# Cross-attention into a maxout FFN on one core: another order of loads, transposes, G pairs and first-layer slices

## The chip, the cores and the metric

The kernel runs on one core of a Trainium2 chip. The metric is the device time of one execution in microseconds (us); lower is better. Four runs of the kernel before took 165.84 to 167.21 us, with a median of 166.62 us.

## What is computed

The reference in short, for x of shape (8, 8, 512, 64) (batch, head, token, width) and state of shape (8, 8, 32, 64):

```python
a     = softmax(x @ state.T / 8)        # per batch and head: 512 x 32
xread = a @ state                       # 512 x 64
a2    = softmax(state @ x.T / 8)        # 32 x 512
sread = a2 @ x                          # 32 x 64
y     = concat([xread, sread])          # per batch 544 rows, heads side by side: 512 columns
h     = max(y @ w1, y @ w2, y @ w3)     # each w is 512 x 768
out   = h @ w_out                       # 4352 x 512, float32
```

## The kernel before, in words

**A rewrite of the first layer.** For the token rows, `xread @ w` is computed as `a @ (state @ w)`. The product `state @ w`, called G, is made per batch by `g_cols` (L230, matmuls L239). One call makes G for one or two of the six 128-column slices m of d_ff; a slice covers the three weights, so it has 384 columns for each of two groups g of heads. Each slice goes into one PSUM tile of tag `two` and is copied to SBUF by ScalarE (L245), or later, when it is deferred into `copies_due` (the copy is then taken up inside the next `maxout`, L265).

**A batch b** passes through these helpers. `load_x` (L68) brings x as bf16 through POOL's queue. The transpose of x is made by TensorE (`x_transpose`, L143) or by a DMA transpose on SP's queue (`x_transpose_dma`, L155). `scores` (L159) multiplies it with the block-diagonal states `bd` into a PSUM tile of tag `two` (or two halves of tag `pw`), and ScalarE takes the exponential (L176) straight out of that tile. `softmax` (L178) is a sum and a reciprocal on VectorE (L183, L185) and a multiply on POOL or VectorE (L186). The transpose of a is again TensorE's (`a_transpose`, L191) or a DMA's (`a_transpose_dma`, L200). `sread` (L207) makes the state rows. `x_maxout(b, m)` (L270, through `maxout`, L253) is one first-layer slice: six matmuls of 128x512 into three PSUM tiles of tag `pw` (L260), a copy of the first to SBUF by ScalarE (L264), and two maxima by VectorE with the second and the third (L267, L268). `ffn_out(b, j)` (L280) is the second layer for a quarter of the tokens: six matmuls into one `pw` tile (L285), a ScalarE copy (L292) and, after each second quarter, an output DMA. `s_maxout` (L275) is the first layer for the state rows of all batches, done beside batch 7.

**PSUM.** The pool has two buffers for tag `two`, [128, 1024] float32 [...], and four for tag `pw`[...]. The tile framework makes the first matmul into a buffer wait until the engine that reads the buffer's former tile has finished.

**Order.** The order on every engine is the order of the program text (`manual_schedule`). First comes a start-up with the loads (L56 to L107) and filler matmuls (`keep_busy`). Then comes the dual phase, in which batches 0 and 1 advance together while the weights arrive: their order is written out by hand, and it ends with G of batch 2 complete and two of batch 0's `ffn_out` quarters done. Then follows a loop over b = 2 to 7: `x_maxout(b, m)` for m = 0 to 5, and after each slice m the work in `slots[m]`: the preparation of batch n = b+1 and the `ffn_out` quarters that are still pending. At the end come the last quarters of batch 7 and of the state rows. The POOL queue carries the loads of x (from batch 1 on), of the weights and of states 1 to 3, most output DMAs, and POOL's softmax multiplies, all in program order; the SP queue carries the DMA transposes.

Lines that the change and the prediction touch:

```python
chunks = ((0, 1), (1, 3), (3, 6))                                    # d_ff slices of a weight load
pp = ctx.enter_context(tc.tile_pool(name="pp", bufs=2, space=bass.MemoryType.PSUM))
p = pp.tile([128, J, n, HS, Ns], F32, tag="two", name="ps")          # scores
p = pp.tile([128, 2, 512], F32, tag="two", name="pg")                # G
p = pp.tile([128, 512], F32, tag="pw", bufs=4, name=f"pw{i}")        # first layer
```

Of the kernel before, what the change touches and what calls it, by code (L numbers as in the profile page):

```python
# [8 lines left out]
F32 = mybir.dt.float32  # L9
BF16 = mybir.dt.bfloat16  # L10
# [5 lines left out]
def kernel(  # L16
# [14 lines left out]
    nc = tc.nc  # L31

    B, H, S, D = x.shape
# [19 lines left out]
    ctx.enter_context(tc.manual_schedule())  # L53

# [29 lines left out]
    for b in range(B):  # L84
        nc.gpsimd.memset(x_sb[b][:, XW:XW + D], 1.0)

    chunks = ((0, 1), (1, 3), (3, 6))
# [3 lines left out]
    def load_w(c):  # L91
        m0, m1 = chunks[c]
        for i, w in enumerate((moe_w1, moe_w2, moe_w3)):
            nc.gpsimd.dma_start(  # L94
                out=w_sb[c][:, :, i, :],
                in_=w.rearrange("(kk p) f -> p kk f", p=128)[:, :, m0 * 128:m1 * 128])
# [6 lines left out]
    load_w(0)  # L103
    bds = [data.tile([128, 2, H, 2, Ns], BF16, name=f"bd{k}") for k in range(B // 2)]
    nc.vector.memset(bds[0], 0.0)
    load_x(1)
    load_w(1)  # L107
# [19 lines left out]
    def states(k, copy):  # L127

        p = pp.tile([128, 4, 128], BF16, tag="pw", bufs=4, name="pt")
        for t in range(4):  # L130
            nc.tensor.transpose(p[:, t, :], st[k][:, t].rearrange("p c d -> p (c d)"), ident)  # L131
        for c in range(2):
            r = slice(64 * c, 64 * c + 64)
            copy(out=bds[k][r, :, :, c, :].rearrange("p b h (q t) -> p (b h) q t", t=4),  # L134
                 in_=p[r].rearrange("p t (k q) -> p k q t", q=8))
# [93 lines left out]

    def g_cols(b, ms, copies=(nc.scalar.copy, nc.scalar.copy), defer=(False, False)):  # L230

        for m, copy, wait in zip(ms, copies, defer):
# [47 lines left out]
    def ffn_out(b, j, split=False):  # L280
# [7 lines left out]
        if split:  # L288
            nc.scalar.copy(out=o[:, j, 0:256], in_=p[:, 0:256])
            nc.vector.tensor_copy(out=o[:, j, 256:512], in_=p[:, 256:512])  # L290
        else:
            nc.scalar.copy(out=o[:, j, :], in_=p)  # L292
# [17 lines left out]
    dve, act, pool = nc.vector.tensor_copy, nc.scalar.copy, nc.gpsimd.tensor_copy  # L310
    both = (True, True)
# [11 lines left out]
    load_w(2)  # L323
    load_x(2)
    nc.gpsimd.dma_start(out=wout_sb, in_=moe_w_out.rearrange("(kk p) f -> p kk f", p=128))
    scores(0, 1, 2)
    softmax(0, 1, 2, nc.vector.tensor_mul)
    g_cols(0, (0,))
    keep_busy(4)
    a_transpose(0, 0, act)  # L330
    a_transpose(0, 1, dve)
    x_transpose(1, 0, act)
    x_transpose(1, 1, dve)
    x_maxout(0, 0)
    scores(1, 0, 2)
    softmax(1, 0, 2, nc.gpsimd.tensor_mul)
    for k in range(1, B // 2):
        load_st(k, nc.gpsimd)
    load_x(3)
    sread(0)  # L340
    g_cols(0, (1, 2))
    x_maxout(0, 1)
    g_cols(1, (0, 1), defer=both)
    a_transpose(1, 0, act)
    a_transpose(1, 1, dve)
    x_maxout(0, 2)
    sread(1)
    x_maxout(1, 0)
    g_cols(1, (2,))
    x_maxout(1, 1)  # L350
    g_cols(0, (3, 4), defer=(False, True))
    states_cast(1, pool)
    x_maxout(1, 2)
    x_maxout(0, 3)
    g_cols(1, (3, 4), defer=both)
    x_maxout(0, 4)
    states(1, dve)
    x_transpose(2, 0, dve)
    x_transpose(2, 1, dve)
    x_maxout(1, 3)  # L360
    g_cols(0, (5,), defer=both)
    scores(2, 0, 2)
    softmax(2, 0, 2, nc.gpsimd.tensor_mul)
    x_maxout(1, 4)
    g_cols(1, (5,), defer=both)
    states_cast(2, pool)
    states_cast(3, pool)
    x_maxout(0, 5)
    sread(2)
    x_maxout(1, 5)  # L370
    g_cols(2, (0, 1))
    a_transpose(2, 0, act)
    a_transpose(2, 1, dve)
    ffn_out(0, 0)
    g_cols(2, (2, 3))
    ffn_out(0, 1)
    g_cols(2, (4, 5))
    assert not copies_due


    pending = [(0, 2), (0, 3)] + [(1, j) for j in range(J)]
    for b in range(2, B):
        n = b + 1
        slots = [[] for _ in range(NM)]
        if n < B:
            if n == 3:
                slots[0].append(lambda: x_transpose(n, 0, act))
                slots[0].append(lambda: x_transpose(n, 1, dve))
                slots[3].append(lambda: x_transpose_dma(n + 1))
            elif n + 1 < B:  # L390
                slots[0].append(lambda: x_transpose_dma(n + 1))
            at = 1 if n == 3 else 0
            slots[at].append(lambda: scores(n, 0, 2))
            slots[at].append(lambda: softmax(n, 0, 2, nc.gpsimd.tensor_mul))
            slots[2 if n == 3 else 1].append(lambda: g_cols(n, (0, 1)))
            slots[2].append(lambda: a_transpose_dma(n))
            slots[3].append(lambda: sread(n))
            slots[4].append(lambda: g_cols(n, (2, 3)))
            slots[5].append(lambda: g_cols(n, (4, 5)))
            slots[4].append(late_transposes)  # L400
            if n % 2 and n + 1 < B:
                slots[3].append(lambda: states((n + 1) // 2, act))
            for k in ((4, 5) if n == 3 else (n + 2,)):
                if k < B:
                    slots[0].append(lambda k=k: load_x(k))
# [3 lines left out]
        for m in (1, 2, 3, 4, 5) if len(pending) > 4 else (1, 2, 4, 5):  # L409
            if pending:  # L410
                slots[m].append(lambda t=pending.pop(0): ffn_out(*t))
# [4 lines left out]
        pending += [(b, j) for j in range(J)]  # L416
    assert pending == [(B - 1, j) for j in range(J)]
# [36 lines left out]
```

The softmax here doesn't subtract the row's maximum and nothing guards it: scores larger than these inputs give would overflow.

## Time and profile before

| | |
|---|---|
| median of 4 runs | 166.62 us |
| the profiled execution | 166.23 us, span of the trace 164.4 us, mean TensorE clock 0.985 |
| busy: TensorE, ScalarE, VectorE, POOL | 151.3, 99.1, 95.9, 43.9 us |
| first G matmul (first weight chunk there) | 9.52 us |
| first slice of batch 0, of batch 2 | 13.60 us, 46.48 us |
| first slices of batches 3, 4, 5, 6, 7 | 65.27, 82.68, 99.24, 115.37, 131.50 us |
| last matmul group issued, end of span | about 160.2 us, 164.4 us |

The profile is of one execution. "PE" is TensorE's matmuls, "PEld" its weight loads, "DVE" VectorE, "ACT" ScalarE; L260 is a line of the kernel. In the timeline a line has the start (us), the duration, the engine, the source line, the operation, its operands and how many were merged; in brackets stands the idle time of the engine just before, and what ended it. The modelled end of a matmul runs over the next one's start, so the time that a group takes on TensorE is read from start to start.

### The profile page before, as it was taken

How to read it: one execution, taken by the hardware profiler on the slowest of the kernel's cores; microseconds unless marked ns; L12 is line 12 of the kernel's file. 1: busy time of each engine (PE TensorE's matmuls, PEld its weight loads, DVE VectorE, ACT ScalarE, POOL GpSimd, SP SyncE). 2: the span in 40 equal slices, each digit the busy share in tenths (PEclk: the TensorE clock that was granted, in tenths of full speed). 3: DMA queues.
4: the chain of work that ended last, by engine and by line, in shares of the span. 5: the costliest groups of instructions: out<-in, count | busy, mean ns of one | idle time of the engine just before them, and what ended most of it. 6: DMA issues, size and time to landing. Idle time of an engine off the chain costs nothing.

```text
span 164.4 us, 3569 instructions
## 1 busy us (share of the span) xinstructions
PE 151.3 (92%) x1432; PEld 71.7 (44%) x1449; DVE 95.9 (58%) x162; ACT 99.1 (60%) x158; POOL 43.9 (27%) x64
## 2 busy tenths in 40 slices
PE   7869699988999999999999999999999999999990
PEld 2436244533445444444344434444444466665430
DVE  4766777889418553665548464865586455585001
ACT  3337578366896678853876688648755853333440
POOL 8975550106150601081016101410141010100140
PEclk9969999999999999999999999999999999999998
DMA  4999999800039999269993988560306030030373
GB/s 136 188 172 198 203 201 246 128 7 0 0 121 136 137 252 201 56 113 140 277 154 131 128 188 89 180 193 12 128 0 195 8 130 0 0 132 0 128 236 147
DMA packets 31825, 20.94 MB, mean 127 GB/s; under 512 B 17185, under 2 KB 29345, under 8 KB 31809
## 3 DMA queue, kind: packets, MB, share of 16 engines
q0 software_dynamic: 15632, 15.08, 46.7%
q1 hardware_dynamic: 16176, 5.64, 18.7%
q8 instruction: 11, 0.18, 0.4%
q14 instruction: 6, 0.04, 0.1%
HBM read 15.20 MB, written 8.91 MB: 147 GB/s over the span
## 4 chain that ended last, share of the span: by engine, by line
PE 65%; DVE 11%; ACT 10%; DMA 4%; issue 4%; POOL 4%; DVEq 0%; ACTq 0%; POOLq 0%
PE pw L260 34%; PE po L285 20%; PE pg L239 4%; DVE den L183 4%; DVE t L267 3%; ACT e L176 3%; ACT G L245 3%; DVE ht L268 3%; DMA w<-in_moe_w_dram 3%; PE ps L171 2%; ACT t L264 2%; PE psr L216 2%; DMA out_dram<-osb 1%; POOL a L186 1%; ACT osb L292 1%
## 5 line engine op out<-in xcount | busy, mean ns | idle before, releaser
L260 PE MATMUL pw<-aT,G 128*128 128x512 bf16 x288 | 71.2, 379 | 3.6 <-ACT G L245 1.8
L267 DVE TENSOR_TENSOR t<-t,pw 128x512 bf16<-128x512 bf16 (+1 forms) x54 | 35.1, 650 | 41.6 <-ACT t L264 39.9
L285 PE MATMUL po<-wout,ht 128*128 128x512 bf16 x188 | 47.9, 380 | 0.8
L260 PEld LDWEIGHTS <-G 128*128 128x128 bf16 x288 | 26.8, 98 | 36.3 <-issue 5.1
L245 ACT CAST G<-pg 128x768 bf16<-128x768 f32 x48 | 36.5, 805 | 8.9 <-PE pg L239 8.7
L264 ACT CAST t<-pw 128x512 bf16<-128x512 f32 (+1 forms) x54 | 30.5, 566 | 14.1 <-PE pw L260 12.6
L268 DVE TENSOR_TENSOR ht<-t,pw 128x512 bf16<-128x512 bf16 (+1 forms) x54 | 35.5, 658 | 5.6
L292 ACT COPY osb<-po 128x512 f32<-128x512 f32 x33 | 19.4, 587 | 21.2 <-PE po L285 20.7
L285 PEld LDWEIGHTS <-ht 128*128 128x128 bf16 x204 | 18.4, 97 | 23.6 <-issue 4.7
L301 POOL DMA_DIRECT2D out_dram<-osb x14 | 7.8, 558 | 70.2 <-ACT osb L292 64.5
L186 POOL TENSOR_TENSOR a<-e,rden 128x1024 bf16<-128x1024 bf16 (+1 forms) x8 | 14.4, 1800 | 33.6 <-DVE rden L185 19.9
L239 PE MATMUL pg<-w,bd 64*32 64x384 bf16 x384 | 13.1, 332 | 1.8 <-DMA w<-in_moe_w_dram 1.8
L183 DVE TENSOR_REDUCE den<-e 128x32 f32<-128x1024 bf16 (+1 forms) x9 | 9.9, 1095 | 2.6 <-ACT e L176 2.6
L176 ACT ACTIVATE e<-ps 128x1024 bf16<-128x1024 f32 x7 | 7.2, 1024 | 5.8 <-PE ps L171 5.8
L239 PEld LDWEIGHTS <-bd 64*32 64x32 bf16 x384 | 3.7, 89 | 12.4 <-issue 12.4
L260 PE MATMUL pw<-ats,w 128*128 128x256 bf16 x72 | 8.8, 273 | 0.0
L260 PEld LDWEIGHTS <-w 128*128 128x128 bf16 x72 | 7.0, 98 | 2.1
L116 PE MATMUL idle<-zero 128*128 128x512 bf16 x12 | 5.9, 630 | 1.4 <-DVE zero L80 1.2
L94 POOL DMA_DIRECT2D w<-in_moe_w_dram x9 | 6.8, 771 | 0.0
L69 POOL DMA_DIRECT2D x<-in_x_dram x7 | 6.6, 951 | 0.0
L134 ACT COPY bd<-pt 64x512 bf16<-64x512 bf16 x6 | 3.5, 580 | 4.2 <-PE pt L131 4.1
L171 PEld LDWEIGHTS <-xT 128*128 128x128 bf16 x128 | 4.7, 98 | 2.4 <-DVE xT L153 0.8
(42 smaller groups left out, 64.6 us busy)
## 6 DMA issues: line engine op xcount, KB each, us to landing
out_dram<-osb POOLq DMA_DIRECT2D x14, 512.0 KB, 3.6
x<-in_x_dram POOLq DMA_DIRECT2D x7, 512.0 KB, 9.1
w<-in_moe_w_dram POOLq DMA_DIRECT2D x3, 384.0 KB, 10.2
w<-in_moe_w_dram POOLq DMA_DIRECT2D x3, 256.0 KB, 8.2
wout<-in_moe_w_out_dram POOLq DMA_DIRECT2D x1, 768.0 KB, 16.3
x0f<-in_x_dram SPq DMA_DIRECT2D x1, 512.0 KB, 3.8
out_dram<-osb SPq DMA_DIRECT2D x1, 512.0 KB, 2.7
out_dram<-osb SPq DMA_DIRECT2D x2, 256.0 KB, 2.1
```

Source lines behind the costliest of these rows:

```text
L171: nc.tensor.matmul(p[:, 2 * jj:2 * jj + 2, g - g0, s, :], xT[b][:, h, jj, :], bd(b, h).rearrange("p c n -> p (c n)"), start=(g == g0 and s ...
L176: nc.scalar.activation(out=e[b][:, :, g0:g1], in_=p, func=AF.Exp, scale=scale)
L183: nc.vector.reduce_sum(out=den, in_=e[b][:, :, g0:g1], axis=AX.X)
L186: mul(out=a[b][:, :, g0:g1].rearrange("p j g s n -> p j (g s) n"), in0=e[b][:, :, g0:g1].rearrange("p j g s n -> p j (g s) n"), in1=rden.r ...
L239: nc.tensor.matmul(p[32 * s:32 * s + 32, g, 0:384].rearrange("p (i f) -> p i f", i=3), bd(b, 2 * s + g)[64 * g:64 * g + 64, g, :], w[64 * ...
L245: copy(out=G[b][:, :, m * 384:(m + 1) * 384], in_=p[:, :, 0:384])
L260: nc.tensor.matmul(p[:, 0:n], lhs(i, k), rhs(k), start=(k == 0), stop=(k == nk - 1))
L264: nc.scalar.copy(out=t0[:, 0:n], in_=pw[0][:, 0:n])
L267: nc.vector.tensor_max(t1[:, 0:n], t0[:, 0:n], pw[1][:, 0:n])
L268: nc.vector.tensor_max(ht[b][:, m, :], t1[:, 0:n], pw[2][:, 0:n])
L285: nc.tensor.matmul(p, ht[b][:, m, j * 128:(j + 1) * 128], wout_sb[:, m, :], start=(m == 0), stop=(m == NM - 1))
L292: nc.scalar.copy(out=o[:, j, :], in_=p)
```

## The change

The weights come in four chunks instead of three, of 1, 1, 2 and 2 slices, and x of batch 1 is loaded before any of them. Of the second chunk one weight is issued early and two behind the first POOL multiply; the third and fourth chunk stand on POOL's queue behind batch 1's first multiply. The dual phase is written in another order: batch 1's scores and softmax come in halves ahead of the first slice, batch 0 has all four of its `ffn_out` quarters done before the loop, and batch 2 enters the loop with two of its six G slices. In the loop `g_cols(b, (2, 3))` (one copy on ScalarE, one on VectorE) follows the scores in slot 0, `g_cols(b, (4, 5))` stands in slot 2, and `g_cols(n, (0, 1))` with `sread(n)` in slot 4. The `softmax` moves to slot 1. Batch 3's transpose of x, batch 2's transpose of a, and the transposes of states 2 and 3 are done by DMA instead of TensorE; POOL copies those states into `bd`. The last quarter of batch 7 goes out as two separate half tiles, one by ScalarE's DMA queue and one by SP's. `g_cols` first carries out copies that are still deferred.

```diff
...
@@ -81,16 +82,16 @@
     ident = const.tile([128, 128], BF16, name="ident")
     make_identity(nc, ident)
     nc.gpsimd.dma_start(out=x0_sb[1], in_=x0_heads(1))
-    for b in range(B):
-        nc.gpsimd.memset(x_sb[b][:, XW:XW + D], 1.0)
-
-    chunks = ((0, 1), (1, 3), (3, 6))
+    load_x(1)
+
+    chunks = ((0, 1), (1, 2), (2, 4), (4, 6))
     w_sb = [wpool.tile([128, HS, 3, (m1 - m0) * 128], BF16, name=f"w{m0}") for m0, m1 in chunks]
     wout_sb = wpool.tile([128, NM, d_model], BF16, name="wout")
 
-    def load_w(c):
+    def load_w(c, parts=(0, 1, 2)):
         m0, m1 = chunks[c]
-        for i, w in enumerate((moe_w1, moe_w2, moe_w3)):
+        for i in parts:
+            w = (moe_w1, moe_w2, moe_w3)[i]
             nc.gpsimd.dma_start(
                 out=w_sb[c][:, :, i, :],
                 in_=w.rearrange("(kk p) f -> p kk f", p=128)[:, :, m0 * 128:m1 * 128])
@@ -101,10 +102,11 @@
         return w_sb[c], slice(f, f + 128)
 
     load_w(0)
+    for b in range(B):
+        nc.gpsimd.memset(x_sb[b][:, XW:XW + D], 1.0)
+    load_w(1, (0,))
     bds = [data.tile([128, 2, H, 2, Ns], BF16, name=f"bd{k}") for k in range(B // 2)]
     nc.vector.memset(bds[0], 0.0)
-    load_x(1)
-    load_w(1)
 
     warm = const.tile([128, 1], F32, name="warm")
     nc.scalar.activation(out=warm, in_=zero[:, 0:1], func=AF.Exp, scale=1.0)
@@ -126,9 +128,13 @@
 
     def states(k, copy):
 
-        p = pp.tile([128, 4, 128], BF16, tag="pw", bufs=4, name="pt")
-        for t in range(4):
-            nc.tensor.transpose(p[:, t, :], st[k][:, t].rearrange("p c d -> p (c d)"), ident)
+        if k < 2:
+            p = pp.tile([128, 4, 128], BF16, tag="pw", bufs=4, name="pt")
+            for t in range(4):
+                nc.tensor.transpose(p[:, t, :], st[k][:, t].rearrange("p c d -> p (c d)"), ident)
+        else:
+            p = data.tile([128, 4, 128], BF16, name=f"stT{k}")
+            nc.sync.dma_start_transpose(out=p, in_=st[k].rearrange("p t c d -> p (t c d)"))
         for c in range(2):
             r = slice(64 * c, 64 * c + 64)
             copy(out=bds[k][r, :, :, c, :].rearrange("p b h (q t) -> p (b h) q t", t=4),
@@ -227,8 +233,13 @@
 
     copies_due = []
 
+    def flush_copies():
+        while copies_due:
+            copies_due.pop(0)()
+
     def g_cols(b, ms, copies=(nc.scalar.copy, nc.scalar.copy), defer=(False, False)):
 
+        flush_copies()
         for m, copy, wait in zip(ms, copies, defer):
             if m == 0:
                 new(G, b, [128, 2, NM * 384], "G", bufs=3)
@@ -286,10 +297,14 @@
                              start=(m == 0), stop=(m == NM - 1))
         o = osb[b]
         if split:
-            nc.scalar.copy(out=o[:, j, 0:256], in_=p[:, 0:256])
-            nc.vector.tensor_copy(out=o[:, j, 256:512], in_=p[:, 256:512])
-        else:
-            nc.scalar.copy(out=o[:, j, :], in_=p)
+            halves = [work.tile([128, d_model // 2], F32, tag=f"oh{k}", bufs=1, name="oh") for k in range(2)]
+            rows = out[b * SP:b * SP + S, :].rearrange("(p j) f -> p j f", j=J)[:, j, :]
+            act(out=halves[0], in_=p[:, 0:256])
+            nc.scalar.dma_start(out=rows[:, 0:256], in_=halves[0])
+            dve(out=halves[1], in_=p[:, 256:512])
+            nc.sync.dma_start(out=rows[:, 256:512], in_=halves[1])
+            return
+        act(out=o[:, j, :], in_=p)
         if b == "s":
             for k in range(4 * j, 4 * j + 4):
                 r0 = k * SP + S
...
@@ -320,101 +333,97 @@
     x_transpose(0, 1, dve)
     scores(0, 0, 1)
     softmax(0, 0, 1, nc.gpsimd.tensor_mul)
-    load_w(2)
-    load_x(2)
-    nc.gpsimd.dma_start(out=wout_sb, in_=moe_w_out.rearrange("(kk p) f -> p kk f", p=128))
+    load_w(1, (1, 2))
     scores(0, 1, 2)
     softmax(0, 1, 2, nc.vector.tensor_mul)
-    g_cols(0, (0,))
     keep_busy(4)
+    x_transpose(1, 0, act)
+    x_transpose(1, 1, dve)
     a_transpose(0, 0, act)
     a_transpose(0, 1, dve)
-    x_transpose(1, 0, act)
-    x_transpose(1, 1, dve)
+    g_cols(0, (0,))
+    scores(1, 0, 1)
+    scores(1, 1, 2)
+    softmax(1, 0, 1, nc.gpsimd.tensor_mul)
+    load_w(2)
+    softmax(1, 1, 2, nc.vector.tensor_mul)
+    load_w(3)
+    load_st(1, nc.gpsimd)
+    load_x(2)
     x_maxout(0, 0)
-    scores(1, 0, 2)
-    softmax(1, 0, 2, nc.gpsimd.tensor_mul)
-    for k in range(1, B // 2):
+    g_cols(0, (1,))
+    g_cols(1, (0,))
+    sread(0)
+    a_transpose(1, 0, act)
+    a_transpose(1, 1, dve)
+    x_maxout(0, 1)
+    nc.gpsimd.dma_start(out=wout_sb, in_=moe_w_out.rearrange("(kk p) f -> p kk f", p=128))
+    for k in range(2, B // 2):
         load_st(k, nc.gpsimd)
     load_x(3)
-    sread(0)
-    g_cols(0, (1, 2))
-    x_maxout(0, 1)
-    g_cols(1, (0, 1), defer=both)
-    a_transpose(1, 0, act)
-    a_transpose(1, 1, dve)
+    x_maxout(1, 0)
+    g_cols(0, (2, 3), (act, dve))
+    sread(1)
+    g_cols(1, (1,), defer=(True,))
     x_maxout(0, 2)
-    sread(1)
-    x_maxout(1, 0)
-    g_cols(1, (2,))
     x_maxout(1, 1)
-    g_cols(0, (3, 4), defer=(False, True))
+    g_cols(1, (2, 3), defer=(False, True))
+    x_maxout(0, 3)
     states_cast(1, pool)
+    g_cols(0, (4, 5), defer=(False, True))
     x_maxout(1, 2)
-    x_maxout(0, 3)
-    g_cols(1, (3, 4), defer=both)
     x_maxout(0, 4)
-    states(1, dve)
+    states(1, act)
     x_transpose(2, 0, dve)
-    x_transpose(2, 1, dve)
+    x_transpose(2, 1, act)
+    x_maxout(0, 5)
+    g_cols(1, (4, 5), defer=(False, True))
     x_maxout(1, 3)
-    g_cols(0, (5,), defer=both)
+    x_transpose_dma(3)
     scores(2, 0, 2)
+    ffn_out(0, 0)
+    x_maxout(1, 4)
     softmax(2, 0, 2, nc.gpsimd.tensor_mul)
-    x_maxout(1, 4)
-    g_cols(1, (5,), defer=both)
-    states_cast(2, pool)
-    states_cast(3, pool)
-    x_maxout(0, 5)
+    a_transpose_dma(2)
+    ffn_out(0, 1)
+    load_x(4)
+    for k in range(2, B // 2):
+        states_cast(k, pool)
+    x_maxout(1, 5)
     sread(2)
-    x_maxout(1, 5)
     g_cols(2, (0, 1))
-    a_transpose(2, 0, act)
-    a_transpose(2, 1, dve)
-    ffn_out(0, 0)
-    g_cols(2, (2, 3))
-    ffn_out(0, 1)
-    g_cols(2, (4, 5))
-    assert not copies_due
-
-
-    pending = [(0, 2), (0, 3)] + [(1, j) for j in range(J)]
+    ffn_out(0, 2)
+    ffn_out(0, 3)
+
+
     for b in range(2, B):
         n = b + 1
         slots = [[] for _ in range(NM)]
         if n < B:
-            if n == 3:
-                slots[0].append(lambda: x_transpose(n, 0, act))
-                slots[0].append(lambda: x_transpose(n, 1, dve))
-                slots[3].append(lambda: x_transpose_dma(n + 1))
-            elif n + 1 < B:
+            if n + 1 < B:
                 slots[0].append(lambda: x_transpose_dma(n + 1))
-            at = 1 if n == 3 else 0
-            slots[at].append(lambda: scores(n, 0, 2))
-            slots[at].append(lambda: softmax(n, 0, 2, nc.gpsimd.tensor_mul))
-            slots[2 if n == 3 else 1].append(lambda: g_cols(n, (0, 1)))
+            slots[0].append(lambda: scores(n, 0, 2))
+            slots[1].append(lambda: softmax(n, 0, 2, nc.gpsimd.tensor_mul))
             slots[2].append(lambda: a_transpose_dma(n))
-            slots[3].append(lambda: sread(n))
-            slots[4].append(lambda: g_cols(n, (2, 3)))
-            slots[5].append(lambda: g_cols(n, (4, 5)))
-            slots[4].append(late_transposes)
             if n % 2 and n + 1 < B:
-                slots[3].append(lambda: states((n + 1) // 2, act))
-            for k in ((4, 5) if n == 3 else (n + 2,)):
-                if k < B:
-                    slots[0].append(lambda k=k: load_x(k))
+                slots[2].append(lambda: states((n + 1) // 2, pool))
+            slots[5].append(late_transposes)
+            if n + 2 < B:
+                slots[0].append(lambda: load_x(n + 2))
         else:
             for m in range(NM):
                 slots[m].append(lambda m=m: s_maxout(m))
-        for m in (1, 2, 3, 4, 5) if len(pending) > 4 else (1, 2, 4, 5):
-            if pending:
-                slots[m].append(lambda t=pending.pop(0): ffn_out(*t))
+        slots[0].append(lambda: g_cols(b, (2, 3), (act, dve)))
+        slots[2].append(lambda: g_cols(b, (4, 5)))
+        if n < B:
+            slots[4].append(lambda: sread(n))
+            slots[4].append(lambda: g_cols(n, (0, 1)))
+        for j, m in enumerate((1, 2, 4, 5)):
+            slots[m].insert(0, lambda j=j: ffn_out(b - 1, j))
         for m in range(NM):
             x_maxout(b, m)
             for f in slots[m]:
                 f()
-        pending += [(b, j) for j in range(J)]
-    assert pending == [(B - 1, j) for j in range(J)]
     ffn_out(B - 1, 0)
     ffn_out(B - 1, 1)
     ffn_out("s", 0)
```

More of the change, by code (lines that the diff above doesn't have):

```diff
@@ L53 @@
     ctx.enter_context(tc.manual_schedule())
+    dve, act, pool = nc.vector.tensor_copy, nc.scalar.copy, nc.gpsimd.tensor_copy
     def load_st(k, eng):
@@ L308, in late_transposes @@
             late.pop(0)()
-    dve, act, pool = nc.vector.tensor_copy, nc.scalar.copy, nc.gpsimd.tensor_copy
-    both = (True, True)
     keep_busy(5)
```

## The prediction

> **What bounds the kernel now.** I read the page first (busy times, then the slices of the span), then TensorE's timeline stage by stage, then all engines around the repeating gaps, then POOL's timeline and the DMA issues.
>
> ```profile
> PE 151.3 (92%) x1432; PEld 71.7 (44%) x1449; DVE 95.9 (58%) x162; ACT 99.1 (60%) x158; POOL 43.9 (27%) x64
> ...
> PE   7869699988999999999999999999999999999990
> ```
>
> TensorE is busy 92% and close to full from the tenth slice of the span on, so time is won only by taking work off it or closing its gaps, and every new wait of TensorE costs in full. Timeline, batch 5, all engines:
>
> ```profile
> 99.24 1.46 PE L260 MATMUL pw<-aT,G 128*128 128x512 bf16 x6
> ...
> 100.54 0.63 PE L171 MATMUL ps<-bd,xT 128*128 128x64 bf16 x16
> ...
> 101.27 1.02 ACT L176 ACTIVATE e<-ps 128x1024 bf16<-128x1024 f32 x1 [0.75 <-PE ps L171]
> ...
> 102.32 1.22 DVE L183 TENSOR_REDUCE den<-e 128x32 f32<-128x1024 bf16 x1 [0.29 <-ACT e L176]
> ...
> 104.65 0.69 DVE L268 TENSOR_TENSOR ht<-t,pw 128x512 bf16<-128x512 bf16 x1
> ...
> 105.39 0.59 PE L260 MATMUL pw<-aT,G 128*128 128x512 bf16 x2 [0.20 <-DVE ht L268]
> ```
>
> A batch takes 16.13 us here (99.24 to 115.37). The only gap is 0.39: four of slice 2's six matmuls start at 104.15, at 0.215 each the last two could run at 105.00, but their `pw` buffer comes free when VectorE, late behind the sum, ends at 105.34. The rest, 15.74, is work: six slices and four quarters of 1.30 each, three G pairs of 0.45, scores 0.46, sread 0.56, and about 0.1 where the operation changes.
>
> The second evidence is the end of the dual phase:
>
> ```profile
> 44.63 1.51 ACT L245 CAST G<-pg 128x768 bf16<-128x768 f32 x2
> ...
> 45.90 0.65 PE L239 MATMUL pg<-w,bd 64*32 64x384 bf16 x16
> ...
> 46.19 0.11 PEld L239 LDWEIGHTS <-bd 64*32 64x32 bf16 x7 [0.18 <-issue]
> ```
>
> Two G slices were to be made. The first started, the second waited until ScalarE's second copy ended at 46.14: both `two` buffers were in use. TensorE cannot make a third `two` tile before the oldest is read out.
>
> [...]
>
> ```profile
> out_dram<-osb POOLq DMA_DIRECT2D x14, 512.0 KB, 3.6
> ...
> aT<-a SPq DMA_TRANSPOSE x5, 4.3
> xT<-x SPq DMA_TRANSPOSE x4, 6.5
> ```
>
> The five aT landings were 4.3, 7.5, 8.0, 3.0 and 3.1 us, the long ones where a load of x was issued at the same moment. [...]
>
> **The change, part by part.** All sums are against the profiled execution (span 164.4).
>
> *1. Start.* With x of batch 1 ahead, the first weight chunk lands about 3.2 us later (x of batch 1 took from 9.4 to 12.6): at 12.6 instead of 9.4. That is covered in part: batch 1's transposes (1.1) and a's are done meanwhile. G, its copy (0.8), then slice (0,0) at 13.9 instead of 13.60. But VectorE now has batch 1's two half softmaxes (0.69 + 0.25, 0.63 + 0.25 + 0.88) ahead of this slice's maxima: they begin at 17.3 instead of 14.88, so slice (0,1) starts at 18.9 (17.97 before), though with batch 1's a transposed, which was so at 20.8 before.
>
> *2. Loads.* POOL multiplied at 9.53 and then issued the third chunk:
>
> ```profile
> 9.53 1.05 POOL L186 TENSOR_TENSOR a<-e,rden 128x512 bf16<-128x512 bf16 x1 [0.98 <-DVE rden L185]
> ...
> 10.53 2.30 POOL L94 DMA_DIRECT2D w<-in_moe_w_dram  x3
> ```
>
> Now that chunk stands behind batch 1's multiply (about 15.5 to 16.55), while the queue is drained at about 15.8. A 512 KB output lands in 3.6 and takes 2.75 at the 190 GB/s of the loads, so 0.9 is lead: transfer starts at 17.5, 768 KB end at 21.6. TensorE wants slices 2 and 3 at 21.6 as well. Hidden, with nothing to spare; a microsecond later costs a microsecond. The fourth chunk (25.8) and x of batch 2 (29) are early enough.
>
> *3. Rest of the dual phase.* I went through the text with the row prices, an engine starting an operation when its input, its own queue and the PSUM buffer allow. ScalarE's copies are the usual hold-up (G(1,1) costs 0.8 at slice (1,1), G(0,5) 0.5, the transposes of batch 2 another 1). Slice (1,5) begins at 41.7, the last `ffn_out` of batch 0 is issued by 46.65. Batch 2's sum stands behind slice (1,4)'s maxima (end 42.0): 1.23 + 0.35, POOL's 1.91, end 45.5. Before, TensorE transposed a in 0.46; now a DMA does. It lands in 3.0 to 8.0 (all five seen); x of batch 4 and an output are issued at the same moment, and I take the mean, 5.2: 50.75. TensorE, empty at 46.65, waits 4.1. Start of the loop: 50.75 against 46.48, **+4.3**. (Before had two quarters fewer done, but four G slices more and a transposed: worth 47.7 on equal work.)
>
> *4. The loop*, time 0 at the first matmul of slice (b,0). Gains: batch 3's transposes (1.5 with its stall), states 2 and 3 (0.25 each and a 0.2 stall) and the 0.39 gaps leave TensorE. New waits:
> (a) Scores run from 1.30 to 1.76 and hold one `two` buffer until the exponential ends at 3.05 (0.73 from scores to its start, 1.02 long). G(b,2) takes the other buffer at once, G(b,3) must wait until 3.1, when it could run at 2.1. Slice (b,1) starts at 3.34: **1.03** lost. In the old order a slice stood between.
> (b) The quarter in slot 2 is issued at 7.24, then the G pair at 8.64, then slices 3 and 4 with nothing between them. ScalarE: output copy 8.73 to 9.32, the two G copies to 10.85, only then slice 3's copy, to 11.47; VectorE's maxima follow, ending at 12.98. Slice 4 and the next quarter need these `pw` buffers: the quarter starts at 13.03 instead of 11.69, **1.34** lost.
> (c) The same behind slot 4's pair (copies end at 16.9) leaves **0.2** at the next slice 0.
> Period 15.74 + 2.57, or 18.25 on my table; five batches 91.25 against 85.02 before: **+6.2**. Moving one G copy of six to VectorE eases ScalarE's total (11.8 to 11.0 of a batch) but none of these chains. The later softmax (multiply ends at 9.7, aT by 12.7 to 17.7) still meets 18.25. POOL's states copies stand behind a DMA transpose and should end near 17, before the scores at 19.5.
>
> *5. Batch 7.* Four G slices come in (0.9 and 0.2 for changes of operation). The pair in slot 2 holds slice 3's copy as in (b): 0.7 and 0.4, and 0.2 at the start. About **+2.3** (before: 19.52 and the fourth quarter, 1.30).
>
> *6. End.* The VectorE half started at 160.69, just as ScalarE's half ended (160.28 + 0.37). If separate tiles part the two, 0.4 is saved; if the shared PSUM tile is what orders them, only the issue changes. I take **−0.2** (0 to −0.4).
>
> Sum: 4.3 + 6.2 + 2.3 − 0.2 = +12.6, span 177.0, execution 178.8; the median of the runs is 0.4 above the profiled execution, so about 179.
>
> Bounds: the aT landing −2.2 to +2.8; waits (a) to (c) 2.0 to 3.0 a batch, ∓2.5; the load gap −0.5 to +2; end ±0.2. Together roughly 174 to 184.
>
> **Rivals.**
> - *The loop's waits are partly absorbed and aT is in time* (172 to 175): POOL's multiply would have to end by 42, or G's copies find ScalarE idle. Without the 4.1 the sum is +8.5, 175; with (b) halved, 172. For it: VectorE's timeline has slack elsewhere. Against it: the queues are in order, and 46.19 shows the wait.
> - *TensorE's work decides, so it is faster* (about 162): if exponential and G copies always ended before TensorE returned to their buffers, the loop would be five times 15.8, its start 46.65, the last batch +1.1. That is 0.2 − 6.0 + 1.1 − 0.2 = −4.9. It turns at the single point where the exponential ends within 0.1 us after G(b,2); the trace has 1.0.
> - *Transfers collide* (184 to 188): every aT at 8 us, or a states transpose that makes scores late by 2 us in batches 2 and 4, or the third chunk 2 us late: +5 to +9 more. For it: landings of 8.0 and 8.7 occur. Against it: only batch 2's aT is on the path with no slack.
> - *Nothing measurable*, within 1% (about what a measurement of this kernel can tell from no change): gains and waits would have to cancel.
>
> **How the numbers follow.** Likeliest case 0.62 (174 to 184), absorbed 0.14, collisions 0.11, faster 0.08, the same 0.05. Slower by over 1%: 0.87. The range takes in the likeliest and most of the absorbed case: 171 to 184.
>
> **What would show it.** G(b,3) starting at the exponential's end in batches 2 to 6, with the slice-to-slice period near 18.2; a gap of about 1.3 before slot 4's quarter with ScalarE in G copies; slice (2,0) waiting for the aT transpose near 50; no TensorE transposes after batch 2. The prediction is wrong if the period stays below 16.5, or if slice (2,0) starts before 47.

## The result, and the profile after

The changed kernel is slower: 179.21 us in the median of 12 runs (176.56 to 181.40) against 166.66 us of 17 runs before, ratio 1.0671 (95% interval 1.0617 to 1.0726). The profiled execution took 179.08 us with a span of 177.3 us (164.4 before). Ratios leave out the executions that took over 1.5% longer than the fastest of their kernel, so they can lie below the quotient of the medians, and of the run `ps_halves`, whose profiled execution was such a one, only the period is read from the profile.

The page of the changed kernel, the lines that answer to those shown of before (engine busy time and share; then the busy tenths and TensorE's granted clock in 40 slices of 4.4 us):

```profile
PE 152.8 (86%) x1397; PEld 72.0 (41%) x1417; DVE 100.7 (57%) x167; ACT 91.7 (52%) x149; POOL 49.7 (28%) x71
...
PE   7876649999947798979898998899899999999991
...
PEclk9999956999996999999999999999999999999999
```

TensorE has 32 matmuls fewer to do (the transposes that went to the DMA) and is busy longer, 152.8 us instead of 151.3, which is 86% of the longer span instead of 92%. It stands still from 20.5 to 24.7 us and from 50.6 to 54.1 us; in both places the granted clock, the share of the full TensorE clock that was let through, falls to 0.50 (from 23 to 29.5 us and from 54 to 57 us). In the loop behind them some slices are at 8 tenths, where before all were at 9. TensorE's timeline shows the places (in brackets the idle time before the group and what ended it):

```profile
24.67 0.84 PE L250 MATMUL pg<-w,bd 64*32 64x384 bf16 x16 [4.16 <-DMA w<-in_moe_w_dram]
...
54.14 2.72 PE L271 MATMUL pw<-aT,G 128*128 128x512 bf16 x6 [3.54 <-DMA aT<-a]
```

The first is the wait for the third weight chunk (batch 0's G pair (2, 3)), the second the one of slice (2,0) for batch 2's DMA transpose. Then batch 3, which stands for all of batches 3 to 6:

```profile
73.04 1.52 PE L271 MATMUL pw<-aT,G 128*128 128x512 bf16 x6
74.40 0.63 PE L177 MATMUL ps<-bd,xT 128*128 128x64 bf16 x16
74.95 0.36 PE L250 MATMUL pg<-w,bd 64*32 64x384 bf16 x8
76.20 0.36 PE L250 MATMUL pg<-w,bd 64*32 64x384 bf16 x8 [0.89 <-ACT e L182]
...
82.22 1.90 PE L271 MATMUL pw<-aT,G 128*128 128x512 bf16 x8
84.41 1.31 PE L271 MATMUL pw<-aT,G 128*128 128x512 bf16 x4 [0.29 <-ACT t L275]
85.56 1.24 PE L296 MATMUL po<-wout,ht 128*128 128x512 bf16 x5
...
90.56 1.52 PE L271 MATMUL pw<-aT,G 128*128 128x512 bf16 x6
```

The second G slice of the pair starts 1.25 us after the first instead of 0.22, when the exponential (L182) has read the scores' buffer: 1.03 lost. In slices 3 and 4 eight matmuls go through, then two waits follow (83.95 to 84.41, and 0.29 inside the last group): 0.75 lost. From slice (3,0) to (4,0) it is 17.52 us, where the kernel before took 16.13 for a batch with the same work (batch 5).

Where the 12.9 us of span lie: the start of slice (2,0) moved from 46.48 to 54.14 (+7.7), the five batches from there to slice (7,0) take 88.98 instead of 85.02 (+4.0), batch 7 takes 22.5 instead of 20.8 (+1.6; the fourth quarter of batch 6, which came behind the loop before, is counted in), the end 11.7 instead of 12.1 (−0.4).

### The profile page after: what moved, and what is told of

Its sections match the earlier page's. It is cut to its first block, busy times and chain, and to the rows that moved or that the text cites. A ratio compares the mean times of both kernels' runs of the same rounds, so it can differ in the third digit from the quotient of the medians.

```text
span 177.3 us, 3523 instructions
## 1 busy us (share of the span) xinstructions
PE 152.8 (86%) x1397; PEld 72.0 (41%) x1417; DVE 100.7 (57%) x167; ACT 91.7 (52%) x149; POOL 49.7 (28%) x71
## 4 chain that ended last, share of the span: by engine, by line
PE 61%; ACT 11%; DVE 10%; DMA 8%; issue 5%; POOL 3%; ACTq 0%; DVEq 0%; POOLq 0%
PE pw L271 31%; PE po L296 21%; PE pg L250 4%; DMA w<-in_moe_w_dram 4%; ACT G L256 4%; ACT e L182 4%; DVE t L278 3%; DMA aT<-a 3%; ACT t L275 2%; PE psr L222 2%; DVE den L189 2%; PE ps L177 2%; POOL a L192 2%; ACT osb L307 1%; DMA stf<-in_state_dram 1%
## 5 line engine op out<-in xcount | busy, mean ns | idle before, releaser
L271 PE MATMUL pw<-aT,G 128*128 128x512 bf16 x288 | 73.7, 390 | 6.6 <-DMA aT<-a 3.5
L296 PE MATMUL po<-wout,ht 128*128 128x512 bf16 x184 | 46.6, 379 | 0.7
L256 ACT CAST G<-pg 128x768 bf16<-128x768 f32 x41 | 31.4, 804 | 11.6 <-PE pg L250 11.6
L275 ACT CAST t<-pw 128x512 bf16<-128x512 f32 (+1 forms) x54 | 30.2, 573 | 13.7 <-PE pw L271 13.7
L296 PEld LDWEIGHTS <-ht 128*128 128x128 bf16 x204 | 19.8, 98 | 23.7 <-issue 0.3
L192 POOL TENSOR_TENSOR a<-e,rden 128x1024 bf16<-128x1024 bf16 (+1 forms) x8 | 13.5, 1692 | 55.6 <-DVE rden L191 43.9
L250 PE MATMUL pg<-w,bd 64*32 64x384 bf16 x384 | 14.3, 340 | 9.6 <-DMA w<-in_moe_w_dram 4.9
L256 DVE CAST G<-pg 128x768 bf16<-128x768 f32 x7 | 6.7, 957 | 8.4 <-PE pg L250 8.4
L95 POOL DMA_DIRECT2D w<-in_moe_w_dram x12 | 9.1, 773 | 0.0
L182 ACT ACTIVATE e<-ps 128x1024 bf16<-128x1024 f32 x6 | 6.1, 1024 | 5.1 <-PE ps L177 5.1
L140 POOL COPY bd<-stT 64x512 bf16<-64x512 bf16 x4 | 4.2, 1062 | 10.6 <-DMA stT<-st 10.5
## 6 DMA issues: line engine op xcount, KB each, us to landing
wout<-in_moe_w_out_dram POOLq DMA_DIRECT2D x1, 768.0 KB, 13.7
```

Source lines behind the costliest of these rows:

```text
L95: nc.gpsimd.dma_start(out=w_sb[c][:, :, i, :], in_=w.rearrange("(kk p) f -> p kk f", p=128)[:, :, m0 * 128:m1 * 128])
L182: nc.scalar.activation(out=e[b][:, :, g0:g1], in_=p, func=AF.Exp, scale=scale)
L192: mul(out=a[b][:, :, g0:g1].rearrange("p j g s n -> p j (g s) n"), in0=e[b][:, :, g0:g1].rearrange("p j g s n -> p j (g s) n"), in1=rden.r ...
L250: nc.tensor.matmul(p[32 * s:32 * s + 32, g, 0:384].rearrange("p (i f) -> p i f", i=3), bd(b, 2 * s + g)[64 * g:64 * g + 64, g, :], w[64 * ...
L256: copy(out=G[b][:, :, m * 384:(m + 1) * 384], in_=p[:, :, 0:384])
L271: nc.tensor.matmul(p[:, 0:n], lhs(i, k), rhs(k), start=(k == 0), stop=(k == nk - 1))
```

## The experiments

All ratios are to the kernel before, run on the same chip; the changed kernel has 1.0671.

**One cost of the changed kernel undone at a time.** Five runs, of which two undo the same cost in different ways. The profiled execution of the changed kernel is the longest of the six in its ratio (spans 174.7 to 177.3), so a difference of spans to it comes out larger than the difference of ratios. The place of a slice and the period of a batch are read within one execution.

`a2_tensor`: batch 2's a transposed by TensorE.

```diff
-    a_transpose_dma(2)
...
     ffn_out(0, 2)
+    a_transpose(2, 0, act)
+    a_transpose(2, 1, dve)
     ffn_out(0, 3)
```

> The changed kernel, but batch 2's a is transposed by TensorE again (between batch 0's third and fourth output quarter). My theory: the wait for the DMA transpose ahead of slice (2,0), 3.5 us and then about 1.2 us at half clock, is paid by nothing else; slice (2,0) starts near 51 instead of 54.1 and the span falls from 177.3 to about 173 (-4 to -5, 0.975 of the changed kernel). Rival (another transfer or the clock would hold slice (2,0) anyway): less than 1.5 us.

Measured 175.74 us, ratio 1.0589 (1.0536 to 1.0642), span 173.5. Slice (2,0) starts at 51.75 and nothing takes the wait's place:

```profile
49.99 0.62 PE L203 MATMUL pat<-ident,a 128*128 128x128 bf16 x8
50.45 1.46 PE L296 MATMUL po<-wout,ht 128*128 128x512 bf16 x6
51.75 1.46 PE L271 MATMUL pw<-aT,G 128*128 128x512 bf16 x6
53.04 0.63 PE L177 MATMUL ps<-bd,xT 128*128 128x64 bf16 x16
```

The slice also takes 1.29 us here, where the changed kernel needed 2.51 behind its wait. So what the rival supposed, that something else would hold the slice, does not happen. The size is less sure: the span's 3.8 us is just short of what the theory said, but the ratio gives 0.8% of 166 us, or 1.4 (0.1 to 2.6, estimated from the two intervals), which is within what the rival allowed.

`w2_early`: the third chunk issued behind the second.

```diff
     load_w(1, (1, 2))
+    load_w(2)
...
     softmax(1, 0, 1, nc.gpsimd.tensor_mul)
-    load_w(2)
```

> The changed kernel, but the third weight chunk is issued right after the second, ahead of batch 1's first POOL multiply. My theory: the chunk was late because of its place in POOL's queue (issued at 15.8, wanted by TensorE at 20.4); issued at 12.3 it lands by about 20.5, the 4.2 us wait at 24.67 goes, and with it about 2.2 us of half clock: span about 171.5 (-5 to -6.5). Rival (the transfers behind x of batch 1 and small chunks are simply slower, so that the chunk lands late wherever it is issued): the wait stays over 2 us and the span falls by less than 3.

Measured 175.00 us, ratio 1.0526 (1.0440 to 1.0612), span 172.9. The wait is gone, but only 3.05 of its 4.16 us arrive at slice (1,5) (42.39 instead of 45.44). TensorE's timeline shows why:

```profile
18.64 4.44 PE L271 MATMUL pw<-aT,G 128*128 128x512 bf16 x12 [0.83 <-ACT aT L204]
23.01 0.52 PE L250 MATMUL pg<-w,bd 64*32 64x384 bf16 x16
```

The twelve matmuls of slices (0,1) and (1,0) start 0.9 later than in the changed kernel and take 4.4 us instead of 2.6: this execution has a stretch at half clock all the same (granted 0.50 from 19 to 22 us), only ahead of the pair. That is no fixed cost of the early load: in `all_four` below, with the same loads, the same twelve start at 18.70 and have a duration of 2.75 us in the timeline instead of 4.44. The cause of the wait (the place in POOL's queue) is shown; that the low clock would go with it is not. By the ratio the gain is 2.4 us, about half of what I expected.

`g23_later`: the pair (2, 3) away from the scores.

```diff
-        slots[0].append(lambda: g_cols(b, (2, 3), (act, dve)))
...
+        slots[1].insert(0, lambda: g_cols(b, (2, 3), (act, dve)))
```

> The changed kernel, but in the loop the G pair (2, 3) stands behind slice (b,1), ahead of the output quarter, instead of right behind the scores. My theory: the pair waited 0.9 to 1.0 us for the exponential to read the scores' buffer in each of batches 2 to 6, which goes, so the period falls from 17.52 to about 16.5 and the span by about 5 us. Rival (the time is given back: the later pair delays slice (b,2), or VectorE or ScalarE is the next bound): period above 17.1, gain below 2 us.

Measured 173.18 us, ratio 1.0425 (1.0367 to 1.0484), span 171.7. The period is 16.44 (slice (3,0) at 71.09, (4,0) at 87.53): 1.08 less, the whole wait, and nothing gives it back.

`ps_halves`: the same wait taken away without moving anything. The scores lie in two buffers of tag `pw`, so that both of tag `two` are free for the G pair; the order stays.

```diff
-            slots[0].append(lambda: scores(n, 0, 2))
+            slots[0].append(lambda: scores(n, 0, 1))
+            slots[0].append(lambda: scores(n, 1, 2))
```

> The changed kernel, but the scores of batches 3 to 7 are made and read out in two halves [...]; the order of the work is unchanged. My theory (the wait of G(b,3) is for the buffer that the exponential reads): the 0.9 us wait goes although the pair still follows the scores, period 17.52 to about 16.6, span about -4.5. Rival (the order on ScalarE's queue is what counts: the exponential ahead of the G copy and slice 1's copy): the same time turns up at slice (b,1), and the period stays above 17.2.

Measured 173.40 us, ratio 1.0419 (1.0362 to 1.0476).

```profile
74.61 0.63 PE L177 MATMUL psh<-bd,xT 128*128 128x64 bf16 x16
75.17 0.52 PE L250 MATMUL pg<-w,bd 64*32 64x384 bf16 x16
75.62 1.47 PE L271 MATMUL pw<-aT,G 128*128 128x512 bf16 x6
```

The pair runs in one piece right behind the scores, and the period is 16.44 (73.25 to 89.69), as in `g23_later`. So the wait was for the buffer; ScalarE's order alone costs nothing here.

`g45_ahead`: the pair (4, 5) ahead of the quarter.

```diff
-        slots[2].append(lambda: g_cols(b, (4, 5)))
...
+        slots[2].insert(0, lambda: g_cols(b, (4, 5)))
```

> The changed kernel, but in the loop the G pair (4, 5) stands ahead of the output quarter in slot 2 instead of behind it. My theory: ScalarE then does the two G copies during the quarter, the copies of slices 3 and 4 are no longer late, and the two waits inside slice 4 (0.46 and 0.29 us by the trace) go: about 0.75 in each of six batches, period 16.8, span -3.5 to -4.5. Rival (two slices in a row are VectorE-bound in any case, 1.48 us of maxima against 1.30): the wait stays above 0.4 and the span falls by less than 2.

Measured 175.05 us, ratio 1.0512 (1.0430 to 1.0593), span 171.6.

```profile
77.37 0.52 PE L250 MATMUL pg<-w,bd 64*32 64x384 bf16 x16
77.82 1.47 PE L296 MATMUL po<-wout,ht 128*128 128x512 bf16 x6
79.13 2.75 PE L271 MATMUL pw<-aT,G 128*128 128x512 bf16 x12
81.72 1.24 PE L296 MATMUL po<-wout,ht 128*128 128x512 bf16 x5
```

Twelve matmuls in one piece: slices 3 and 4 take 2.59 us instead of 3.34, and the period is 16.79 (69.93 to 86.72), 0.73 less. VectorE's pace, the rival, does not show. By the ratio the gain is 2.6 us (1.0 to 4.3, estimated from the two intervals), where five such periods and batch 7 would give about 4 (an estimate).

**Together.** `all_four` has the four edits `a2_tensor`, `w2_early`, `g23_later` and `g45_ahead`.

> The changed kernel with all four edits at once (a of batch 2 transposed by TensorE, third weight chunk early, pair (2, 3) behind slice (b,1), pair (4, 5) ahead of the quarter). My theory: the four costs are separate, so the gains add up: slice (2,0) near 48, five periods of 15.7, last batch 21.8, span about 160, time about 161.5, that is 0.97 of the kernel before. Rival (the costs hide one another, as one engine's queue is the bound behind all of them): the span stays above 164.5 and the kernel is no faster than before.

Measured 163.47 us, ratio 0.9824 (0.9776 to 0.9871), span 161.6: faster than the kernel before, though by less than 2%, and 1.6 us of span short of the expectation. A cost came to light that the four waits had covered:

```profile
64.78 0.63 PE L177 MATMUL ps<-bd,xT 128*128 128x64 bf16 x16 [0.97 <-POOL bd L140]
...
97.77 0.63 PE L177 MATMUL ps<-bd,xT 128*128 128x64 bf16 x16 [1.01 <-POOL bd L140]
```

The scores of batches 4 and 6 wait for POOL, which copies the DMA-transposed states. All engines, the same kernel:

```profile
59.13 1.28 SPq L137 DMA_TRANSPOSE stT<-st  x1
...
62.55 2.17 POOL L140 COPY bd<-stT 64x512 bf16<-64x512 bf16 x2 [5.87 <-DMA stT<-st]
```

From the issue to the end of the copies it is 5.6 us; TensorE and ScalarE did it in 0.25 and 1.17.

`states_pe`: `all_four` with states 2 and 3 by TensorE.

```diff
-        if k < 2:
+        if True:
             p = pp.tile([128, 4, 128], BF16, tag="pw", bufs=4, name="pt")
...
-                slots[2].append(lambda: states((n + 1) // 2, pool))
...
+            slots[5].insert(0, lambda: states((n + 1) // 2, act))
```

> The kernel with all four edits, and states 2 and 3 transposed by TensorE and copied by ScalarE again (behind slice (b,5)), as before the change. My theory: with the four waits gone, the scores of batches 4 and 6 wait 1.0 us each for POOL's copies of the DMA-transposed states; that goes, TensorE pays 0.25 twice: span 161.6 to about 160, 0.97 to 0.975 of the kernel before. Rival (the scores would then wait for their x, transposed by DMA): span unchanged.

Measured 162.55 us, ratio 0.9776 (0.9724 to 0.9828), span 159.6. The two waits are gone; 0.33 us remains at the quarters ahead of slices (3,0) and (5,0), behind ScalarE's copies.

`states_pe_w1`: and the second chunk issued whole.

```diff
-    load_w(1, (0,))
+    load_w(1)
...
-    load_w(1, (1, 2))
```

> The kernel of the run before it (four edits, states by TensorE), and the second weight chunk issued whole at once instead of one weight early and two behind POOL's first multiply. My theory: the 0.7 to 1.4 us that TensorE waited for this chunk at about 15 us shrinks by 1, and the rest follows: 0.965 to 0.97 of the kernel before. Rival (the stage behind it is bound by VectorE and ScalarE, which have the softmax of batch 1 to do): no gain against the run before it.

Measured 161.71 us, ratio 0.9742 (0.9684 to 0.9799), span 159.5. Slice (2,0) starts at 44.93 instead of 45.97, but a transpose of a is then late once (0.73 ahead of slice (3,0)). Intervals and spans do not part this run from `states_pe`; both are faster than the kernel before and than the changed one.

**The clock.** `clock_filler`: the changed kernel with unused matmuls in its two long waits.

```diff
+    keep_busy(18)
     g_cols(0, (2, 3), (act, dve))
...
     ffn_out(0, 3)
+    keep_busy(15)
```

> The changed kernel with filler matmuls in front of its two long waits (18 before batch 0's G pair (2, 3), 15 before slice (2,0)); they compute nothing that is used. My theory: the waits stay (slice (2,0) still waits for the transpose, the G pair for its weights), but the array is at full clock behind them, where the profile of the changed kernel shows 0.43 instead of 0.215 us a matmul for about 4.5 us and for 1.3 us: 2 to 3.4 us less, about 0.985 of the changed kernel. Rival (the low clock comes with the chip's state and not with the idling): matmuls behind the waits are as slow as before and the time is the same.

Measured 178.50 us, ratio 1.0761 (1.0715 to 1.0807): no gain. Stretches of the changed kernel (the granted clock is the third number from the right):

```profile
22.00:24.00 2.00, 0.00 (x0) 0.00 (x0) 0.00 (x0) 0.00 (x0) 1.12 (x2) 0.75 1.35 177
24.00:26.00 2.00, 1.33 (x40) 0.74 (x44) 0.42 (x1) 0.74 (x1) 0.56 (x1) 0.50 1.45 196
26.00:28.00 2.00, 2.00 (x31) 0.78 (x23) 1.00 (x3) 0.11 (x2) 0.90 (x1) 0.50 1.40 229
```

and of the run with filler:

```profile
24.00:26.00 2.00, 2.00 (x43) 0.88 (x44) 0.12 (x1) 0.29 (x1) 1.25 (x2) 1.00 1.43 192
26.00:28.00 2.00, 1.80 (x42) 0.89 (x30) 1.20 (x3) 1.02 (x3) 0.10 (x2) 1.00 1.39 231
```

The clock stays at 1.00 here, and its mean is 0.997 to 1.00 in all four executions, where the twelve of the changed kernel have 0.961 to 0.989. So in these runs the low clock was gone where the waits were filled. From the G pair to slice (1,5) the work takes 19.4 instead of 20.8 us, and slice (2,0) 1.3 instead of 2.5. It was given back: slices (0,1) and (1,0) began 1.0 later, and batch 2's transpose, issued at 48.46 instead of 49.23, landed in 6.5 instead of 4.8 us, so slice (2,0) started at 55.00, 0.9 later than without filler. What the low clock costs the changed kernel in all is therefore left open. The changed kernel's own executions suggest that it costs something: the three with a mean clock of 0.980 to 0.989 took 176.6 to 176.7 us, the nine with 0.961 to 0.978 took 178.35 to 181.40; no run shows whether the clock is the cause.

Nor does the length of a wait settle, in these runs, how fast TensorE is behind it. In `g23_later` slice (2,0) waits as long as in the changed kernel, and its six matmuls take 1.29 us to the next operation's start, as a slice of the changed kernel does at a granted clock of 1.00 (1.30 at 42.84):

```profile
54.71 1.45 PE L271 MATMUL pw<-aT,G 128*128 128x512 bf16 x6 [3.64 <-DMA aT<-a]
```

`w2_early` (3.63) and `g45_ahead` (3.64) do the same, while a wait of 2.29 us in `before_dma_t` below has a slice of 2.67 us behind it.

**Parts of the change in the kernel before.** `before_g_adjacent` moves the next batch's pair right behind its scores.

```diff
-            slots[2 if n == 3 else 1].append(lambda: g_cols(n, (0, 1)))
+            slots[at].insert(len(slots[at]) - 1, lambda: g_cols(n, (0, 1)))
```

> The kernel before with one thing of the change brought in: in the loop the G pair (0, 1) of the next batch stands right behind its scores instead of behind the next slice. My theory: the second of the pair waits about 1.0 us for the exponential in each of batches 2 to 6, and the 0.39 us gap of the old order goes: +0.6 a batch, +3 us, 1.015 to 1.025. Rival (what the changed loop lost was lost by its later softmax and its G slices made just in time, not by the pair's place): within 0.5% of the kernel before.

Measured 170.45 us, ratio 1.0265 (1.0209 to 1.0322), span 168.2. The same line as in the changed kernel appears, in a kernel with all else as before:

```profile
103.42 0.36 PE L239 MATMUL pg<-w,bd 64*32 64x384 bf16 x8
104.66 0.35 PE L239 MATMUL pg<-w,bd 64*32 64x384 bf16 x8 [0.89 <-ACT e L176]
```

Batch 5 takes 16.84 instead of 16.13: 1.03 for the pair, less most of the 0.39 gap. The ratio is a little above the expected range.

`before_dma_t` has the DMA transposes of x of batch 3 and of states 2 and 3, the latter copied by POOL.

```diff
+        if k < 2:
             p = pp.tile([128, 4, 128], BF16, tag="pw", bufs=4, name="pt")
...
+            nc.sync.dma_start_transpose(out=p, in_=st[k].rearrange("p t c d -> p (t c d)"))
...
+    x_transpose_dma(3)
...
-                slots[0].append(lambda: x_transpose(n, 0, act))
-                slots[0].append(lambda: x_transpose(n, 1, dve))
...
-                slots[3].append(lambda: states((n + 1) // 2, act))
+                slots[3].append(lambda: states((n + 1) // 2, pool))
```

> The kernel before with one part of the change: x of batch 3 and states 2 and 3 transposed by DMA, the states copied by POOL. My theory: TensorE loses 1.5 us for batch 3 and about 0.25 each for the states, with a 0.2 stall, and no DMA is waited for: -2.0 to -2.3, 0.987 of the kernel before. Rival (a transpose is late, or POOL's copies delay the softmax multiplies behind them): 0.995 or more.

Measured 170.65 us, ratio 1.0244 (1.0190 to 1.0297): my theory fell, the rival holds.

```profile
67.18 0.63 PE L175 MATMUL ps<-bd,xT 128*128 128x64 bf16 x16 [1.83 <-POOL bd L138]
...
103.17 0.73 PE L175 MATMUL ps<-bd,xT 128*128 128x64 bf16 x16 [2.29 <-POOL bd L138]
103.72 2.75 PE L264 MATMUL pw<-aT,G 128*128 128x512 bf16 x6
```

The scores of batches 4 and 6 wait for POOL's copies, as in `all_four`, but longer. Behind the second wait the slice takes 2.67 us instead of 1.39, about the pace of slice (2,0) in the changed kernel (2.51 us, granted clock 0.50).

`before_xt3` has the part for x of batch 3 alone (the two `x_transpose` lines out, `x_transpose_dma(3)` in).

> The kernel before with one part of the change: only x of batch 3 is transposed by DMA, the states by TensorE as before. My theory: this is the part of the transposes that pays (1.5 us of TensorE and ScalarE work), and the states' part cost the 4 us that turned the earlier run with both into a loss: 0.990 to 0.993. Rival (the DMA transpose of x is what was late): 1.00 or more.

Measured 165.21 us, ratio 0.9955 (0.9937 to 0.9973), span 163.4. It pays, but less than I said, and the range that I gave does not hold:

```profile
46.35 1.90 PE L260 MATMUL pw<-aT,G 128*128 128x512 bf16 x8
48.45 1.31 PE L260 MATMUL pw<-aT,G 128*128 128x512 bf16 x4 [0.20 <-ACT t L264]
49.60 0.63 PE L171 MATMUL ps<-bd,xT 128*128 128x64 bf16 x16
```

Without the transposes between them, slices (2,0) and (2,1) run back to back behind ScalarE's G copies. They take 3.25 us instead of the 2.60 of two slices, with the pattern that slices 3 and 4 of the changed kernel have; with the transposes it was 4.11. So it is the states' part that turned `before_dma_t` into a loss.

## Why the prediction was right, and where it was not

The direction holds, and so do its reasons in kind: TensorE waits for buffers in the loop and for the DMA transpose at its start. The total holds too (179 said, 179.21 measured; +12.6 of span said, +12.9 measured), but that it came this close is luck: one term, the start of the loop, was too small by 3.4 us, two others, the loop and batch 7, were too large by 2.9 together. The wait for the third weight chunk and the half clock were not in the sum at all.

*Step 1, start.* Slice (0,0) came at 13.10 and (0,1) at 17.76, 0.8 and 1.1 earlier than worked out; TensorE had x of batch 1 at 9.53 and needed no wait for the first chunk at 11.82, which I had put at 12.6. That VectorE's half softmaxes stand ahead of slice (0,0)'s maxima is as said (16.29 instead of 14.88).

*Step 2, loads: failed.* "Hidden, with nothing to spare" was wrong by 4.2 us: about 3 because the chunk was late, 1.1 because TensorE was there at 20.5 and not at 21.6. The issue at 15.77 was near the predicted 15.8; the landing was not. DMA by the microsecond in the changed kernel (last column GB/s):

```profile
17.00:18.00 1.00, 0.62 (x6) 0.38 (x6) 0.90 (x3) 0.71 (x2) 1.00 (x2) 1.00 0.53 30
18.00:19.00 1.00, 1.00 (x6) 0.46 (x5) 0.48 (x2) 0.59 (x1) 1.00 (x3) 1.00 1.14 150
19.00:20.00 1.00, 1.00 (x6) 0.48 (x5) 0.89 (x2) 0.32 (x1) 1.00 (x2) 1.00 1.45 196
20.00:21.00 1.00, 0.51 (x3) 0.01 (x1) 1.00 (x2) 0.27 (x1) 1.00 (x3) 1.00 1.36 159
21.00:22.00 1.00, 0.00 (x0) 0.00 (x0) 0.77 (x2) 0.00 (x0) 1.00 (x2) 1.00 1.29 165
22.00:23.00 1.00, 0.00 (x0) 0.00 (x0) 0.00 (x0) 0.00 (x0) 1.00 (x2) 1.00 1.34 173
23.00:24.00 1.00, 0.00 (x0) 0.00 (x0) 0.00 (x0) 0.00 (x0) 0.12 (x1) 0.50 1.37 182
```

The transfer started about half a microsecond later than I took, and ran at 150 to 196 GB/s, on average 171, instead of 190. By 24.0 us 1.05 MB had been moved, although the chunk has only 0.79 MB: its third part shared the engines with the fourth chunk, issued right behind, and landed at about 24.5. I had counted the queue as strictly one after the other. In `w2_early` the third part was issued at about 13.7 and landed 6.3 us later, at about 20.0, so the place in the queue was the cause.

*Step 3, transpose of a.* Said: TensorE waits 4.1 us, from a landing of 5.2. Measured: 3.54, landing 4.8, everything about 3.4 later, since the dual phase was already late (slice (1,5) at 45.44 instead of 41.7). I had charged nothing for a lower clock. The profiled execution shows a granted 0.50 behind both waits and 1.2 us more for slice (2,0). The other runs show this only in part: behind three waits of 3.63 and 3.64 us a slice took 1.29 us, and behind one of 2.29 it took 2.67, so the length of a wait alone does not tell what comes behind it; what does is not shown.

*Step 4(a)* was exact: 1.03 said and measured, and `ps_halves` shows that it was the buffer. *Step 4(b)* had the right chain and the wrong size, 0.75 instead of 1.34. The term that failed is the last link: I let the quarter behind slice 4 wait for the last maximum of slice 3, as in a strict rotation of the four buffers. It started at 85.56, while VectorE was in that maximum:

```profile
84.39 0.69 DVE L278 TENSOR_TENSOR t<-t,pw 128x512 bf16<-128x512 bf16 x1 [2.24 <-ACT t L275]
85.18 0.69 DVE L279 TENSOR_TENSOR ht<-t,pw 128x512 bf16<-128x512 bf16 x1
```

That maximum ended at 85.87, so the quarter did not wait for its buffer. Of the four buffers this leaves the one of slice 4's first tile, which ScalarE had read by 84.85: the buffers were not taken in strict turn. *Step 4(c)* was 0.06 instead of 0.2, so a batch lost 1.8, not 2.6 (period 17.52, not 18.25). That POOL's states copies end before the scores was right, by as little as 0.3 us in batch 5 (copies to 109.16, scores at 109.44), and only because the other waits delayed the scores: `all_four` and `before_dma_t` show it.

*Step 5*: 1.6 instead of 2.3, with the same too large (b). *Step 6*: 0.4 instead of 0.2. Separate tiles do not part the two halves:

```profile
173.56 0.37 ACT L302 COPY oh<-po 128x256 f32<-128x256 f32 x1 [0.71 <-PE po L296]
173.96 0.37 ACTq L303 DMA_DIRECT2D out_dram<-oh  x1
173.97 0.42 DVE L304 COPY oh<-po 128x256 f32<-128x256 f32 x1 [7.59 <-ACT oh L302]
```

VectorE still starts (173.97) when ScalarE has ended (173.93), and the trace puts the end of its wait down to ScalarE's half. Both read one PSUM tile, the second of the two cases that I had named; no run here tests whether the tile is the reason. What is saved comes behind the copies: from VectorE's end to the end of the span it is 2.9 instead of 3.3 us.

*Rivals.* "TensorE's work decides" and "nothing measurable" did not come about. Of "transfers collide" one part did, the late chunk; the loop's smaller waits balanced it. Of "partly absorbed" one half did, the halved wait (b), but the transpose of a was not in time.

## What to carry to other kernels

When an operation takes one of two PSUM buffers and is read out slowly, leave one more TensorE operation between it and the next pair that needs both (1.08 us a batch here); count the buffers that are unread at that moment, and, where a quarter or slice waits, look up which buffer it really got. Copies that one engine must do in a burst belong ahead of a TensorE operation that needs none of them, not ahead of one that does (0.73 us a batch here). A load that stood behind a compute instruction in its issuing queue was late by that instruction's wait (the third part of the chunk was issued at about 17.3 us here, at 13.7 in `w2_early`), and it shared the engines with what was issued right after it (7.2 us to land here, 6.3 there). Last, undo the waits one at a time and then all together: undone together they showed the cost that they had hidden.

## What was not expected of the hardware

Transfers issued one behind the other from POOL's queue overlapped: the third part of a chunk needed 7.2 us to land with the next chunk right behind it, where the first two needed 4.7 and 5.2; in `w2_early`, with the next load 1.4 us behind it, the three needed 5.1, 5.6 and 6.3. Behind the changed kernel's waits of 4.16 and 3.54 us the work took about 1.4 and 1.2 us longer, at a granted clock of 0.50, and with the waits filled with matmuls the clock stayed at 1.00; but behind three waits of 3.6 us without filler a slice took 1.29 us too, and behind one of 2.29 it took 2.67. POOL's copy of a 64x512 bf16 tile from SBUF took 1.06 us, where ScalarE's from PSUM took 0.58.
